# Preparing the next pair in units -1 to 5, and its conversions two units apart

## The chip, the cores and the metric

The kernel runs on one core of one Trainium2 chip. The metric is device time in microseconds (us): the time of one execution as the device measures it. The engines have short names below: TensorE is PE (its weight loads PEld), VectorE is DVE, ScalarE is ACT, GpSimd is POOL, and SyncE (SP) issues nearly all DMAs of the part that matters here.

## The reference

Three stages run one after the other; the change lies in the first.

```python
# 1. attention: batch 2, 8 heads, 768 rows, head size 64
q_bits = (einsum('bhsd,dk->bhsk', q, proj) > 0)      # 6 bits a row, a bucket number
k_bits = (einsum('bhsd,dk->bhsk', k, proj) > 0)
mask   = q_bucket[..., :, None] == k_bucket[..., None, :]
scores = where(mask, scale * q @ k.T, -1e9)
attn   = softmax(scores) @ v
# 2. mixture of experts: 1536 tokens, 8 experts of 192 tokens each, 512 -> 1024 -> 512
# 3. rms norm, then (silu(xn @ w_gate) * (xn @ w_val)) @ w_out: 512 -> 1536 -> 512
```

The three weight matrices of stage 3 arrive as 64-bit numbers. They are not needed before stage 3, but the kernel turns them into 32-bit numbers during the attention ("conversions").

## The kernel before

**Units and pairs.** The 16 heads of both batches are taken two at a time: eight pairs (0 to 7), each of six row tiles of 128 by two heads, so twelve units a pair and NU = 96 units. A unit is one head's 128 rows against all 768 keys. The loop over u issues a software pipeline: the exponential of unit u+1 (expo, L350, ACT), six transposes of the probabilities of unit u (transp, L361, PE) with their copies out of PSUM (L363 on ACT, L365 on DVE), the scores of unit u+2 (scores, L336 and L339, PE; then the row minimum L341 on DVE), half of the product with v (pv, L380, PE; copy L385, ACT), in even units the combination of a finished tile (comb, L395; comb_v, L420), and at last whatever the table fill holds for this unit. Each engine runs its own instructions in this order of issue, and SP its DMAs too; a wait holds up everything behind it on that engine. So L339 of the first tile of the next pair, issued in unit 10, must find that pair's operands ready.

**Preparing a pair.** For pair p, during pair p-1, the table holds: prep_t four times, for k and q and each half of the rows (three transposes L278, a copy by ACT, L282 or L284, then POOL's rounded part nh, L285, and rest nl, L286); prep_d after the second half of k and of q (six DMAs each, L310 to L312, that put these parts in the layout of the scores); prep_p for each half (six products with the projection, L294, then the sign comparison L297 on DVE into sg); prep_s after the second (four DMAs of the signs, L320); and in the unit behind it load_pair for the next pair but one (three DMAs, L98). SLOTS names the units: -1 and 0 for k, 1 and 3 for q, 5 and 6 for the signs. Pair 1, prepared during pair 0, has its own SLOTS1.

**Conversions.** There are 36, each of a 128 by 512 block: conv_load (one DMA of 512 KB, L242, into the wide buffer w64, of which there are three), conv (one instruction on ACT, L250; two on DVE, L253 and L254; four on POOL, L255 to L258) and conv_store (one DMA of 256 KB, L263). Conversion n stands in unit 5 + 12n/5: units 5, 7 and 9 of pair 0, 0, 2, 5, 7 and 9 of pairs 1 to 6, and 0, 2 and 5 of pair 7. Its load is issued five units earlier and its store three later. Within a unit what belongs to the preparation stands ahead of the conversion.

**PSUM.** The transposes, prep_t, prep_p and comb take their output tiles from one ring of three buffers (ps_m, tile m), so each waits until the copy out of the tile three places back is done.

Behind the attention, the routing of stage 2 begins with key work on DVE and weight splits on ACT; the 32-bit weights are read back much later.

Of the kernel before, what the change touches and what calls it, by code (L numbers as in the profile page):

```python
# [15 lines left out]
I64 = mybir.dt.int64  # L16
# [7 lines left out]
BIG = 2.0 ** 30  # L24
ACT_EVAC = 1
SLOTS1 = (0, 0, 4, 5, 5, 6)
CONV = 5
SLOTS = (-1, 0, 1, 3, 5, 6)
WSTEP = (4, 7, 9, 10, 10, 13, 15, 16)
POOL_LO = (0, 1, 4, 5, 7)  # L30
DVE_HI = (0, 4)
# [15 lines left out]
def lsh_attention__moe__swiglu_kernel(ctx, tc, q, k, v, proj, m_wg, m_w1, m_w2,  # L47
# [8 lines left out]
    TPB = S // 128  # L56
# [29 lines left out]
    cv = att.enter_context(tc.tile_pool(name="cv", bufs=2))  # L86
# [140 lines left out]
    convs = []  # L227
    for src, dst in ((f_wg, wg_d), (f_wv, wv_d), (f_wo, wo_d)):
        n = src.shape[0] * src.shape[1] // (128 * 512)
# [5 lines left out]
    def cv_at(src, i):  # L235
        per = src.shape[1] // 512
        return slice((i // per) * 128, (i // per) * 128 + 128), slice((i % per) * 512, (i % per) * 512 + 512)

    def conv_load(n):
        src, dst, i = convs[n]  # L240
        w = cv.tile([128, 512], I64, name="w64", bufs=3)
        nc.sync.dma_start(w, src[cv_at(src, i)])  # L242
        CV[n] = w

# [266 lines left out]
    def at(u, f, *a):  # L511
        fill.setdefault(u, []).append((f, a))

    for p in range(1, NPAIR):
        u0 = (p - 1) * TPB * 2
        slots = iter(SLOTS if p > 1 else SLOTS1)
        for nm in "kq":
            for half in range(2):
                n = u0 + next(slots)
                at(n, prep_t, p, nm, half)  # L520
            at(n, prep_d, p, nm)
        for half in range(2):
            n = u0 + next(slots)
            at(n, prep_p, p, half)
        at(n, prep_s, p)
        if p + 1 < NPAIR:
            at(n + 1, load_pair, p + 1)
    for n in range(len(convs)):
        u = CONV + n * 12 // 5
        at(u - 5, conv_load, n)  # L530
        at(u, conv, n)
        at(u + 3, conv_store, n)
    for i in range(8):
# [59 lines left out]
    for s in range(2):  # L593
        r = slice(64 * s, 64 * s + 64)
# [718 lines left out]
```

## Time and profile before

| what | value |
|---|---|
| median of 3 runs | 814.34 us (813.39 to 814.79) |
| the profiled execution, time | 814.53 us |
| its span, first to last instruction | 812.7 us |
| PE busy | 761.3 us, 94% |
| DVE / ACT / POOL busy | 513.7 / 398.0 / 328.6 us |
| mean granted clock of TensorE | 0.967 |
| DMA over the span | 115.58 MB, mean 142 GB/s |
| conversion loads, median from issue to landing | 5.3 to 6.4 us |

The span is cut on the page into 40 slices of 20.3 us; the attention takes the first 14 to 15 of them. Busy time of PE counts an instruction from start to modelled end, so a busy PE can still be slowed by its clock. In lists of instructions, "idle before" is the time in which the engine did nothing ahead of that instruction, and the name behind it is what ended that idle time.

### The profile page before, as it was taken

The page shows a single profiled execution, that of the slowest core. Times are in us where ns is not written, and L with a number is a line of the kernel's source. Part 1 is how long each engine was busy: PE and PEld are TensorE (multiplying, and loading weights), DVE is VectorE, ACT ScalarE, POOL GpSimd, SP SyncE. Part 2 cuts the span into 40 slices and gives each one's busy share as a digit, 9 for nine tenths or more (in the row PEclk, how much of TensorE's full clock was granted, in tenths as well). Part 3 has the DMA queues.
Part 4 walks back from the last instruction along what each step waited for, and adds up shares of the span by engine and source line. Part 5 has one row for each costly group of instructions (what it writes and reads, how often), then busy time and mean ns, then how long its engine had stood idle before and what let it go on. Part 6 is the DMA issues. An engine that isn't in the chain of part 4 may idle for free.

```text
span 812.7 us, 14759 instructions
## 1 busy us (share of the span) xinstructions
PE 761.3 (94%) x5317; PEld 685.2 (84%) x5317; DVE 513.7 (63%) x1342; ACT 398.0 (49%) x863; POOL 328.6 (40%) x309
## 2 busy tenths in 40 slices
PE   7999999999989983698999999999999999999997
PEld 3788777787878863498999999999999999999996
DVE  7788786889878878467787887766422332233222
ACT  3677765676766762265676776644211221121111
POOL 3278786877868720586767660000100010001001
PEclk8999999999999995699999999999999999999999
DMA  3578897989879612377777834363200110001001
GB/s 79 175 206 217 258 248 208 271 253 278 213 233 268 192 34 78 96 226 226 244 255 241 261 102 156 117 195 117 78 1 1 40 39 1 1 1 40 1 1 39
DMA packets 89770, 115.58 MB, mean 142 GB/s; under 512 B 22124, under 2 KB 68188, under 8 KB 89692
## 3 DMA queue, kind: packets, MB, share of 16 engines
q1 hardware_dynamic: 87612, 108.28, 44.8%
q0 software_dynamic: 1920, 6.29, 2.1%
q8 instruction: 44, 0.72, 0.4%
q14 instruction: 34, 0.28, 0.1%
q10 hardware_dynamic: 160, 0.00, 0.0%
HBM read 77.62 MB, written 18.87 MB: 119 GB/s over the span
## 4 chain that ended last, share of the span: by engine, by line
PE 37%; issue 18%; POOL 1%; DVE 1%; ACT 1%; POOLq 0%; ACTq 0%; DVEq 0%
PE pg L1194 6%; PE pv L1194 6%; PE py L1029 6%; PE po L1222 6%; PE ph L1005 6%; PE py L1031 3%; PE ph L1007 3%; POOL out_dram L1230 1%; PE ph L983 1%; PE py L1101 0%; DVE wl L218 0%; PE px L1061 0%; PE px L1084 0%; ACT bt L1015 0%; DVE yn L1091 0%
## 5 line engine op out<-in xcount | busy, mean ns | idle before, releaser
L1230 POOL DMA_INDIRECT out_dram<-ot,oi x12 | 11.7, 974 | 307.8 <-DVE ot L1228 306.2
L350 ACT ACTIVATE pr<-sc,rs 128x768 f32<-128x768 f32 x96 | 94.9, 989 | 50.4 <-DVE rs L343 31.6
L341 DVE TENSOR_REDUCE rs<-sc 128x1 f32<-128x768 f32 x96 | 91.5, 953 | 34.7 <-PE sc L339 34.2
L218 POOL TENSOR_TENSOR wl<-wr,wh 128x1024 fp32r<-128x1024 f32 x39 | 95.0, 2446 | 44.0 <-PE ph L983 20.9
L1203 DVE TENSOR_TENSOR a<-sg,pg 128x384 f32<-128x384 f32 x48 | 26.6, 553 | 103.1 <-ACT sg L1201 103.1
L361 PE MATMUL m<-ident,pr 128*128 128x128 f32 x576 | 83.4, 281 | 3.1 <-ACT pt L363 2.5
L380 PE MATMUL xo<-pt,ld_v 128*64 128x128 f32 x1128 | 82.9, 282 | 0.0
L1005 PE MATMUL ph<-xg,wh 128*128 128x384 f32 x256 | 75.3, 363 | 3.8 <-DVE ht L1022 3.1
L1029 PE MATMUL py<-ht,wh 128*128 128x384 f32 x256 | 76.7, 364 | 0.0
L361 PEld LDWEIGHTS m<-ident,pr 128*128 128x128 f32 x576 | 63.8, 141 | 15.1 <-issue 7.4
L380 PEld LDWEIGHTS xo<-pt,ld_v 128*64 128x64 f32 x1128 | 60.0, 137 | 18.6 <-issue 11.9
L1201 ACT ACTIVATE sg<-pg 128x384 f32<-128x384 f32 x48 | 23.5, 490 | 105.8 <-PE pg L1194 105.7
L1207 ACT ACTIVATE ah<-a 128x384 fp32r<-128x384 f32 x48 | 25.2, 525 | 99.3 <-DVE a L1204 99.3
L1194 PE MATMUL pg<-xh,gl 128*128 128x384 f32 x192 | 64.6, 336 | 0.0
L1194 PE MATMUL pg<-xl,gh 128*128 128x384 f32 x192 | 64.5, 336 | 0.0
L1194 PE MATMUL pg<-xh,gh 128*128 128x384 f32 x192 | 64.5, 336 | 0.0
L1194 PE MATMUL pv<-xh,vl 128*128 128x384 f32 x192 | 64.4, 335 | 0.0
L1194 PE MATMUL pv<-xl,vh 128*128 128x384 f32 x192 | 64.4, 335 | 0.0
L1194 PE MATMUL pv<-xh,vh 128*128 128x384 f32 x192 | 64.4, 335 | 0.0
L1031 PE MATMUL py<-ht,wl 128*128 128x192 f32 x256 | 63.7, 253 | 0.0
L215 ACT ACTIVATE wh<-wr 128x1024 fp32r<-128x1024 f32 x50 | 51.2, 1054 | 14.2 <-PE py L1029 11.4
L339 PE MATMUL sc<-s_k,s_q 82*128 82x384 f32 x192 | 49.9, 341 | 8.7 <-DMA s_q<-sg 8.7
(252 smaller groups left out, 1952.4 us busy)
## 6 DMA issues: line engine op xcount, KB each, us to landing
wr<-in_moe_w_dram SPq DMA_DIRECT2D x64, 512.0 KB, 4.7
w<-in_moe_w_gate_dram SPq DMA_DIRECT2D x12, 512.0 KB, 6.4
w<-in_moe_w_val_dram SPq DMA_DIRECT2D x12, 512.0 KB, 5.7
w<-in_moe_w_out_dram SPq DMA_DIRECT2D x12, 512.0 KB, 5.3
s_k<-nh_k SPq DMA_DIRECT2D x28, 192.0 KB, 3.4
s_q<-nh_q SPq DMA_DIRECT2D x28, 192.0 KB, 4.2
ld_v<-in_v_dram SPq DMA_DIRECT2D x8, 384.0 KB, 6.2
wg_d<-ha SPq DMA_DIRECT2D x12, 256.0 KB, 5.5
```

The lines of the kernel that those rows point to most:

```text
L215: nc.scalar.activation(WH[i], WR[i], AF.Copy)
L218: (nc.gpsimd if pool else nc.vector).tensor_tensor(WL[i], WR.pop(i), WH[i], op=OP.subtract)
L339: nc.tensor.matmul(ps[:, n, :HALF], q2[:64 + NS, h, qs], k2[:64 + NS, h, n * HALF:(n + 1) * HALF], start=False, stop=True)
L341: nc.vector.tensor_reduce(rs[:, h, 0:1], ps[:, :, :HALF], axis=AX.XY, op=OP.min)
L350: nc.scalar.activation(pt, ps[:, :, :HALF], AF.Exp, scale=rs[:, h, 1:2], bias=rs[:, h, 2:3], accum_out=rs[:, h, 3:4])
L361: nc.tensor.transpose(t[:, i, :], pt[:, c * 128:(c + 1) * 128], ident)
L380: nc.tensor.matmul(xo[64 * h:64 * h + 64], vt[:, h, chunk(p, c), :], a[h][:, c, :], start=(c == 0), stop=(c == TPB - 1))
L1005: hi = lambda: nc.tensor.matmul(ph[:, :2 * CAP], wh[:, d], xg[:, d].rearrange("p a b -> p (a b)"), start=(d == 0), stop=(d == KD - 1), ski ...
L1029: hi = lambda: nc.tensor.matmul(py[d][:, :2 * CAP], wh[:, ds], ht[:, f].rearrange("p a b -> p (a b)"), start=(f == 0), stop=(f == KF - 1), ...
L1031: lo = lambda: nc.tensor.matmul(py[d][:, :CAP], wl[:, ds], ht[:, f, 0], start=False, stop=False, skip_group_check=True)
L1194: nc.tensor.matmul(t[:, :TJ], a[:, d, :], b_[:, d, :], start=(n == 0), stop=(n == 3 * KD - 1))
L1222: nc.tensor.matmul(PO[j][t], a[:, ts], b_, start=(f == 0 and n == 0), stop=(f == KG - 1 and n == 2))
```

## The change

The preparation moves to units -1, 0, 1 and 2 for the transposes (the second half of q from 3 to 2) and 4 and 5 for the signs (from 5 and 6), and load_pair with it from 7 to 6. SLOTS1 stays. The conversions get a list of units for each pair: four in pairs 0, 1, 3, 5 and 6, five in pairs 2 and 4, six in pair 7, in all 36 as before. Most lie two units apart; in pairs 1, 3, 5 and 6 the first is in unit 3, in pairs 2 and 4 in unit 2. Loads of conversions in units 3 to 7 of a pair are issued two units before that pair begins, the others five units ahead, and none before the unit behind the conversion that last read its buffer; there are four wide buffers.

```diff
-CONV = 5
-SLOTS = (-1, 0, 1, 3, 5, 6)
+CONV1 = (5, 7, 9, 11)
+CONV5 = (2, 4, 6, 8, 10)
+CONV4 = (3, 5, 7, 9)
+CONVN = (0, 2, 4, 5, 7, 9)
+SLOTS = (-1, 0, 1, 2, 4, 5)
...
     def conv_load(n):
         src, dst, i = convs[n]
-        w = cv.tile([128, 512], I64, name="w64", bufs=3)
+        w = cv.tile([128, 512], I64, name="w64", bufs=4)
...
-    for n in range(len(convs)):
-        u = CONV + n * 12 // 5
-        at(u - 5, conv_load, n)
+
+    turns = [CONV1, CONV4, CONV5, CONV4, CONV5, CONV4, CONV4, CONVN]
+    units = [w * TPB * 2 + u for w, t in enumerate(turns) for u in t]
+    assert len(units) == len(convs)
+    for n, u in enumerate(units):
+
+        r = u % (TPB * 2)
+        at(max(u - r - 2 if 3 <= r < 8 else u - 5, units[n - 4] + 1 if n > 3 else 0), conv_load, n)
         at(u, conv, n)
         at(u + 3, conv_store, n)
```

## Rows read from the trace of the kernel before

**Rows 1.** The page's 40 slices of the span, busy share in tenths and granted clock.

```profile
PE   7999999999989983698999999999999999999997
...
PEclk8999999999999995699999999999999999999999
```

**Rows 2.** Table of windows, PE, pairs 1 to 7: stretch, length, busy (count), clock, DMA.

```profile
267.90:294.70 26.80, 26.80 (x256) 1.00 0.35 117
sum 240.00, PE 227.99; mean PE 32.57
```

**Rows 3.** Waits of PE in pairs 1 to 6: us in total, times, longest.

```profile
PE sc L339 <- DMA s_q<-sg: 8.7, 4, 3.0
PE m L361 <- ACT pt L363: 2.5, 6, 0.4
PE m L361 <- ACT nr_k L284: 0.6, 1, 0.6
```

**Rows 4.** Table of windows, PE, behind the wait of pair 2.

```profile
125.00:128.00 3.00, 3.00 (x19) 0.50 1.06 406
```

**Rows 5.** Timeline of PE in pair 2: start, us, instruction, [idle before <- releaser].

```profile
105.48 0.93 PE L361 MATMUL m<-ident,pr 128*128 128x128 f32 x6 [0.42 <-ACT pt L363]
...
112.65 0.82 PE L361 MATMUL m<-ident,pr 128*128 128x128 f32 x6
...
120.40 0.60 PE L336 MATMUL sc<-s_k,s_q 128*128 128x384 f32 x2
123.87 0.59 PE L339 MATMUL sc<-s_k,s_q 82*128 82x384 f32 x2 [2.87 <-DMA s_q<-sg]
```

**Rows 6.** Timeline of DVE in pair 2.

```profile
100.16 1.43 DVE L253 TENSOR_SCALAR ha<-w 128x512 int32<-128x512 int32 x1
101.51 0.72 DVE L254 TENSOR_SCALAR sg<-w 128x512 int32<-128x512 int32 x1
...
109.79 0.42 DVE L253 TENSOR_SCALAR ha<-w 128x512 int32<-128x512 int32 x1
...
112.85 0.68 DVE L297 TENSOR_SCALAR sg<-m,pm 114x384 fp32r<-114x384 f32 x1 [0.46 <-PE m L294]
```

**Rows 7.** Timeline of SP's DMA issues in pair 2.

```profile
108.19 0.60 SPq L310 DMA_DIRECT2D s_q<-nh_q  x1
...
111.74 0.61 SPq L312 DMA_DIRECT2D s_q<-nl_q  x1
...
116.22 1.71 SPq L320 DMA_DIRECT2D s_k<-sg  x2
117.97 1.59 SPq L320 DMA_DIRECT2D s_q<-sg  x2
```

**Rows 8.** Timeline of POOL in pair 2.

```profile
103.28 0.61 POOL L255 TENSOR_SCALAR ha<-ha 128x512 f32<-128x512 f32 x1
...
106.44 1.28 POOL L258 TENSOR_TENSOR ha<-ha,sg 128x512 int32<-128x512 int32 x1
107.66 0.50 POOL L285 CAST nh_q<-nr_q 128x384 fp32r<-128x384 f32 x1
108.24 1.02 POOL L286 TENSOR_TENSOR nl_q<-nr_q,nh_q 128x384 fp32r<-128x384 f32 x1
```

**Rows 9.** Timeline of all engines at the end of pair 5.

```profile
225.56 1.59 SPq L320 DMA_DIRECT2D s_q<-sg  x2
...
232.08 0.59 PE L339 MATMUL sc<-s_k,s_q 82*128 82x384 f32 x2 [3.00 <-DMA s_q<-sg]
```

**Rows 10.** Timeline of all engines at the start of pair 5.

```profile
197.87 1.14 DVE L193 TENSOR_SCALAR kl<-kl 128x48 f32<-128x48 f32 x1
...
199.62 0.52 PE L361 MATMUL m<-ident,pr 128*128 128x128 f32 x3 [0.59 <-ACT nr_k L284]
```

**Rows 11.** Table of windows, the last pair, PE, PEld, DVE, ACT, POOL in turn.

```profile
267.90:294.70 26.80, 26.80 (x256) 22.68 (x254) 22.76 (x76) 20.40 (x46) 15.81 (x15) 1.00 0.35 117
```

**Rows 12.** The page's list of DMA issues: count, size, us to landing.

```profile
w<-in_moe_w_gate_dram SPq DMA_DIRECT2D x12, 512.0 KB, 6.4
```

## The prediction

> **What bounds the kernel now.** I read the slices of the page first: TensorE (PE) is busy in nearly all of the first 14 of 40 slices, the attention, with nine tenths or more of its clock from the second slice on [rows 1]. The change touches attention alone, so the question is how much PE idles there. A table of PE by pair answers: cut at each pair's first exponential, the seven pairs from 1 on take 240.00 us and PE is busy for 227.99; the last one takes 26.80 for 11 units and has no idle time at all [rows 2]. So all 12.01 us of idle time lie in pairs 1 to 6, which take 213.20. A plain unit then costs 26.80 / 11 = 2.44 us and PE sets the pace wherever nothing holds it. PE's waits in the same stretch say what holds it: 8.7 us in four waits for the sign copies (s_q<-sg, L320) before L339, 2.5 us in six waits of 0.42 for a copy out of PSUM, 0.6 us once [rows 3]; together 11.8 of the 12.0.
>
> A wait costs more than itself once: behind the one of 2.87 us the clock, granted in full while PE was busy, fell to 0.50, the lower of its two levels (1.2 GHz), for 3 us [rows 4], and work that takes 3.0 us there takes 1.5 at the upper one, and I count 1.6 with the edges. What can be won is at most 12.0 + 1.6 = 13.6 us.
>
> Now one long wait, in pair 2. Unit 5's transposes start at 105.48, unit 7's at 112.65; at 120.40 unit 10 begins the scores of the next pair and at 121.00 it needs the copied signs, which come at 123.87 [rows 5]. The last sign half was computed by VectorE (DVE) at 112.85 to 113.53 [rows 6], yet SP issued the sign copies only from 116.22 to 119.56: from 108.19 it issues without a pause, first the six copies of q to 112.35, then stores and loads that stand in line before prep_s [rows 7]. SP began so late because the q copies need GpSimd's (POOL's) second q half, and that cast started at 107.66, straight behind a conversion that held POOL from 103.28 to 107.72 [rows 8]. So the cause is conversion, then q casts, then SP, then signs.
>
> **Prep earlier.** The changed slots put the second half of q at unit 2 instead of 3, the sign products at 4 and 5 instead of 5 and 6, and move ten of SP's copies and three loads with them. The number of instructions is the same everywhere. Call the start of unit n T(n). Before, signs were ready 0.88 us after T(7) and PE needed them 121.00 - 112.65 = 8.35 after it. After, they are ready 0.88 after T(6), and PE needs them 8.35 + 2.44 = 10.79 after it. The four issues take 119.56 - 116.22 = 3.34, and the last landed 4.31 after its issue here [rows 5, 7] and 4.93 in the longest wait (232.08 - 227.15) [rows 9]: 8.5 to 9.2 us after T(6), which is 1.6 to 2.3 us early. This needs SP free by then. With no conversion ahead of it in four of the pairs, POOL does the two instructions of the second q half in 1.60 us (107.66 to 109.26) [rows 8]; give ScalarE's (ACT's) copy before them a whole unit, 2.44, then 4.16 for six issues and 0.86 for a load (half of the 1.71 of two sign issues): SP is free 9.1 after T(3) at worst, while T(6) lies 2.44 + 7.17 = 9.6 after T(3). The 8.7 us of waits and the 1.6 of slow clock go. On SP the q copies now stand right behind the two x_d stores of the same unit, which wait for DVE's product of that unit; what that costs them lies within the worst case above. Behind prep_s stands load_pair, which leaves a unit earlier; its first reader is at unit 11. Two or three conversion loads now leave together at unit 10, ahead of the k copies of unit 0, which nobody reads for ten units. So nothing on this chain is late next within 1.6 us.
>
> **Conversions two units apart.** Each conversion is unchanged work: one ACT, two DVE, four POOL instructions. What changes is whom they meet. DVE's first one (L253) took 1.43 us at 100.16, while POOL was inside another conversion, and 0.42 at 109.79, with POOL idle [rows 6, 8]. After that slow case DVE was behind and PE waited 0.42 at 105.48 [rows 5]; that is the wait that comes six times. The slow one is the conversion of unit 2, between the q casts. In the four pairs with units 3, 5, 7, 9 it is gone; pairs 2 and 4 still have one in unit 2, so I keep 2 x 0.42 = 0.8, and 0.6 for the single wait in pair 5, which follows L193 at 1.14 us [rows 10] and has nothing to do with the slots. Retained: 1.4. POOL keeps up: 4.44 us a conversion [rows 8] against two plain units of 4.87.
>
> In words of the Trainium skill ("SBUF — State Buffer", section "Who interferes with whom") VectorE and GpSimd share a port pair as an exclusive lock, and the second to ask waits for the whole instruction of the first. The two L253 durations agree. By that rule each conversion that meets a busy GpSimd could be held twice, once per VectorE instruction; this is the second rival below.
>
> **The last pair.** It had three conversions and gets six, in units 0, 2, 4, 5, 7, 9. DVE is busy 22.76 of 26.80 us there, 4.04 free [rows 11]. Three more cost 3 x 0.84 = 2.5, with both instructions at 0.42. The one in unit 5 follows by 2.44 what holds POOL for 4.44, and those of 7 and 9 then find POOL busy too: three times 2.15 (1.43 + 0.72, by 100.16 and the one after it [rows 6]) in place of 0.84, another 3.9. That is 6.4 against 4.04 free: 2.4 over. If none of the free time can be used it is 6.4, if the three fall in gaps it is 0. I take 2.0, near the first, since DVE can catch up in the gaps before its waits for PE. POOL ends near the pair's end; nothing of the routing waits for it soon.
>
> **Four units of transposes in a row.** Units 11, 0, 1 and 2 each have three transposes more and an ACT copy more; before it was 11, 0, 1 and 3. The trace has three in a row without PE idling, and one place where PE waited 0.59 for such a copy [rows 10]. Bounds: 0, or 6 preparations x 4 x 0.59 = 14.2 (pair 1 keeps SLOTS1). I take 0.5, since the three in a row cost nothing. The fourth wide buffer and the earlier loads change no engine's work, and I take them at nothing: every conversion's load is issued five to nine units ahead, 12 us or more, where it was always five, and a load lands 6.4 us after its issue [rows 12]. Were one late, L250 would hold ACT, and the exponential behind it, for as long.
>
> **Sum.** 13.6 - 1.4 - 2.0 - 0.5 = 9.7 us less. The profiled execution took 814.53 (span 812.7), so 804.8; the median of the runs shown is 814.34, 0.2 below, so **804.6 us**. About 0.2%, 1.6 us, is what a measurement here can tell from no change.
>
> **Rivals.**
> Copies still late (0.10): the sign copies land later than 4.93 after issue because loads were put ahead of them. For it: a wide load lands 6.4 after issue [rows 12]; at 7.5 the copies come 11.7 after T(6), 0.9 late in each of six pairs, 5.5 us: 810. Against: only one wide load stands between the q copies and the signs now. The Trainium skill ("DMA: Bandwidth & Descriptors", section "Queues, rings and completion order") says each DMA engine takes descriptors in the order of its ring, which is why bytes queued ahead count; landing at 4.31 and 4.93 does not settle how much.
>
> The last pair pays (0.13): DVE is held by POOL in both instructions of the three crowded conversions and its free time is not usable: 6.4 instead of 2.0, 809. For it: DVE has 4.04 free of 26.80 [rows 11]. Against: the pair's own three conversions before cost PE nothing.
>
> All costs vanish (0.06): 13.6 less, 801 or below.
>
> No change (0.06): the signs come early but PE then waits as long elsewhere, say for the next pair's first copies, 812.7 to 816. Against: no other wait in the rows is near 8.7 us.
>
> Slower (0.07): with four transposing units in a row PE finds no free PSUM buffer, since ACT has its exponential, its copies and the new one in each. Place: units 11 to 2; price: 0.59 each [rows 10], 24 times 14.2 us, in all 814.3 - 13.6 + 1.4 + 2.0 + 14.2 = 818.3. The gain is used up at 10.2 / 0.59, some 17 of the 24, and from 20 on it is slower by more than 0.2%. Against: units 11, 0 and 1 in a row made PE wait in no pair but the fifth [rows 3].
>
> My forecast has 0.58, for 801 to 807.5. Faster is 0.58 + 0.10 + 0.13 + 0.06 = 0.87, within 0.2% 0.06, slower 0.07. A range of 800.8 to 811.0 takes in the forecast and the two rivals above it; it leaves out the gain's edge, no change and slower, 0.19.
>
> **What would show it.** Right: no wait of PE on L339 for s_q<-sg over 0.3 us; prep_s issued by SP about 1 us after the second L297, with a pause before it; six pairs near 33 us; L253 near 0.42 but in the last pair and in unit 2; no stretch at 0.50 before the attention's end. Wrong: L339 still waits; PE waits for nr_k or nr_q copies or for pt in units 11 to 5; the last pair over 29 us; ACT held at L250 by a load that is not there.

## The result and the profile after

The changed kernel takes **801.74 us** (median of 4 runs, 800.46 to 801.89) where the kernel before took 813.87 (813.26 to 814.79): a ratio of 0.9847, 95% interval 0.983 to 0.9864. That is 12.1 us less. The forecast was 804.6, in a range of 800.8 to 811.0; the sign is right, the gain larger than said. The profiled execution took 801.59 us, its span is 799.7 (before 812.7), so the two traces differ by 13.0. In experiments 2, 3 and 9 below, one run each took 858 to 932 us at a lower mean clock (0.75 to 0.83); the ratios leave it out, and it moves the medians by at most 0.4 us. Code lines of the attention stand three lower in the changed file: L339 is now L342, L361 is L364, L250 (ACT) is L253, L253 (DVE) is L256, L297 is L300, L320 is L323.

The slices of the page, which answer to [rows 1], no longer have the 8 in the twelfth slice, where the wait at the end of pair 5 was [rows 9]:

```profile
PE   7999999999999954889999999999999999999997
...
PEclk9999999999999975899999999999999999999999
```

The table of windows by pair (stretch, length, PE busy with count, clock, DMA share, GB/s) answers to [rows 2, 11]; of the seven stretches these are the fifth pair, the last, and the sum:

```profile
186.20:220.40 34.20, 33.27 (x304) 1.00 0.84 256
...
253.10:281.50 28.40, 26.85 (x254) 1.00 0.43 150
sum 226.60, PE 224.03; mean PE 32.00
```

PE's idle time in these pairs went from 12.01 us to 226.60 - 224.03 = 2.57, and 1.55 of it lies in the last pair. What is left has other names than in [rows 3] (PE's waits, us in total, times, longest):

```profile
PE m L364 <- DVE pt L368: 2.1, 2, 1.2
PE m L364 <- ACT pr L353: 0.3, 1, 0.3
```

In these stretches no wait for the sign copies remains and none above 0.1 us for ACT's copies out of PSUM, and the clock is 1.00 in all seven stretches. Cut more finely, from one unit's first transpose (L364) to the next's, the 13.0 us come from these places:

| place | before | after | difference |
|---|---|---|---|
| unit 10, six pairs (the wait for the signs, and the start of the slow clock in pair 2) | 26.33 | 15.31 | -11.0 |
| units 2 to 6, six pairs | 92.8 | 88.7 | -4.2 |
| unit 11, six pairs (rest of the slow clock in pair 2: 3.73 to 2.69) | 17.56 | 16.83 | -0.7 |
| all other units of the six pairs | 76.4 | 76.9 | +0.5 |
| last pair, 11 units | 26.19 | 28.55 | +2.4 |

Pair 2 again, SP and then PE, answering to [rows 7, 5]:

```profile
105.45 0.61 SPq L315 DMA_DIRECT2D s_q<-nl_q  x1
106.16 0.75 SPq L245 DMA_DIRECT2D w<-in_moe_w_gate_dram  x1
108.42 1.71 SPq L323 DMA_DIRECT2D s_k<-sg  x2
110.18 1.60 SPq L323 DMA_DIRECT2D s_q<-sg  x2
```

```profile
107.51 0.82 PE L364 MATMUL m<-ident,pr 128*128 128x128 f32 x6
...
118.25 0.51 PE L342 MATMUL sc<-s_k,s_q 82*128 82x384 f32 x2
```

Here SP is done with the q copies at 106.06 and pauses from 106.91 to 108.42, until the signs exist. The last of the four issues ends 111.78 - 107.51 = 4.27 us after unit 6 began, and L342 starts 10.74 after it, without a wait. Pairs 4, 5 and 6 are like this. In pair 3 the last issue ends 4.9 us after unit 6 began, and in pair 1, where POOL's k casts stand behind the conversion of unit 11 of pair 0, 7.5 us after it; L342 does not wait there either.

Most of the last pair's loss, 1.84 of 2.36 us, is in one place. DVE and POOL around its unit 6, and PE behind them:

```profile
269.91 1.28 POOL L260 TENSOR_TENSOR ha<-ha,lr 128x512 int32<-128x512 int32 x1
270.11 1.37 DVE L256 TENSOR_SCALAR ha<-w 128x512 int32<-128x512 int32 x1
...
271.26 1.35 POOL L261 TENSOR_TENSOR ha<-ha,sg 128x512 int32<-128x512 int32 x1
271.39 1.50 DVE L257 TENSOR_SCALAR sg<-w 128x512 int32<-128x512 int32 x1
...
273.42 0.55 PE L364 MATMUL m<-ident,pr 128*128 128x128 f32 x3 [1.24 <-DVE pt L368]
...
275.79 0.44 PE L364 MATMUL m<-ident,pr 128*128 128x128 f32 x2 [0.32 <-ACT pr L353]
```

The conversion of unit 5 meets that of unit 4 on POOL. Both DVE instructions start just behind the start of a POOL instruction and last 1.37 and 1.50 us in place of 0.42 each; DVE's copy L368 comes late, and PE's unit 7 takes 4.15 us where it took 2.31. The other 0.5 us come at the pair's end.

### The profile page after: what moved, and what is told of

It is laid out like the page before. It is cut to its first block, busy times and chain, and to the rows that moved or that the text cites. A ratio compares the mean times of both kernels' runs of the same rounds, so it can differ in the third digit from the quotient of the medians.

```text
span 799.7 us, 14773 instructions
## 1 busy us (share of the span) xinstructions
PE 758.3 (95%) x5317; PEld 685.1 (86%) x5317; DVE 510.5 (64%) x1342; ACT 397.9 (50%) x863; POOL 329.5 (41%) x309
## 4 chain that ended last, share of the span: by engine, by line
PE 37%; issue 18%; DVE 1%; POOL 1%; ACT 1%; POOLq 0%; ACTq 0%; DVEq 0%
PE pg L1202 6%; PE pv L1202 6%; PE py L1037 6%; PE po L1230 6%; PE ph L1013 5%; PE py L1039 3%; PE ph L1015 3%; POOL out_dram L1238 1%; PE ph L991 1%; PE py L1109 0%; DVE wl L221 0%; PE px L1069 0%; PE px L1092 0%; ACT bt L1023 0%; ACT sq L1055 0%
## 5 line engine op out<-in xcount | busy, mean ns | idle before, releaser
L1238 POOL DMA_INDIRECT out_dram<-ot,oi x12 | 11.7, 977 | 307.7 <-DVE ot L1236 306.2
L364 PE MATMUL m<-ident,pr 128*128 128x128 f32 x576 | 82.1, 278 | 2.9 <-DVE pt L368 2.1
L364 PEld LDWEIGHTS m<-ident,pr 128*128 128x128 f32 x576 | 63.4, 140 | 13.7 <-issue 5.3
L218 ACT ACTIVATE wh<-wr 128x1024 fp32r<-128x1024 f32 x50 | 51.1, 1053 | 13.8 <-PE py L1037 11.4
L366 ACT ACTIVATE pt<-m 128x384 f32<-128x384 f32 x120 | 55.7, 487 | 4.1 <-PE m L364 3.7
```

The costliest lines, as they stand in the source:

```text
L218: nc.scalar.activation(WH[i], WR[i], AF.Copy)
L364: nc.tensor.transpose(t[:, i, :], pt[:, c * 128:(c + 1) * 128], ident)
L366: nc.scalar.activation(o[:, 3 * half:3 * half + 3, :], t, AF.Copy)
```

## The experiments

Each run is shown with its edit. Every time is a median and stands beside the kernel before on the same chip, whose medians lie between 814.9 and 816.3.

**1. The slots alone** (kernel before, new SLOTS).

```diff
-SLOTS = (-1, 0, 1, 3, 5, 6)
+SLOTS = (-1, 0, 1, 2, 4, 5)
```

> The kernel before with the new slots alone; its conversions stay in units 0, 2, 5, 7 and 9, with three wide buffers. Order theory (the second half of q now stands ahead of the conversion of unit 2 in GpSimd's queue, and the signs a unit earlier, so the copies of the signs arrive before PE asks for them): the waits on s_q<-sg are gone, 12 us, the short waits behind the conversion of unit 2 stay, the last pair loses nothing: 801 to 803. Spacing theory (only conversions kept out of the preparation free GpSimd and VectorE): the conversion of unit 0 still stands ahead of the q casts, SP stays late, half or more of the waits stay: 808 or above.

Measured: 804.18 us, ratio 0.9861 (0.9829 to 0.9892), a little over what was expected. PE's waits in the pairs:

```profile
PE m L294 <- ACT pt L363: 2.6, 5, 0.5
PE m L361 <- ACT nr_k L284: 0.6, 1, 0.6
```

The signs are never late. But the crowded conversion is still there (POOL's last conversion instruction, then DVE's two):

```profile
99.16 1.28 POOL L258 TENSOR_TENSOR ha<-ha,sg 128x512 int32<-128x512 int32 x1
99.28 1.45 DVE L253 TENSOR_SCALAR ha<-w 128x512 int32<-128x512 int32 x1
...
100.65 0.72 DVE L254 TENSOR_SCALAR sg<-w 128x512 int32<-128x512 int32 x1
```

Unit 4 takes 4.33 us here and 3.71 after the whole change, in every pair: 0.62 x 6 = 3.7 us that only the new places of the conversions win. The last pair stays at 26.19.

**2. The conversions alone** (changed kernel, old SLOTS).

```diff
-SLOTS = (-1, 0, 1, 2, 4, 5)
+SLOTS = (-1, 0, 1, 3, 5, 6)
```

> The changed kernel with the old slots (second half of q in unit 3, signs in 5 and 6); conversions two units apart. Order theory: signs are 0.88 us after unit 7 begins, copied 8.5 to 9.2 us after it, wanted 8.35 after it: 0.2 to 0.9 us late in the four pairs with conversions in 3, 5, 7, 9, and 1.5 to 3.7 in the two with one in unit 2, which again stands ahead of the q casts. With 0.3 us of PE time more at each wait than its idle time shows: 6 to 11 us above the changed kernel, 808 to 812. Spacing theory: no waits, 801 to 803.

Measured: 804.53 us, ratio 0.9863 (0.9826 to 0.9899), between the two expectations and nearer to the lower, so I was wrong here: this half alone is worth as much as the other. PE's waits name the signs once:

```profile
PE m L364 <- DVE pt L368: 1.8, 2, 1.2
PE sc L342 <- DMA s_q<-sg: 1.5, 1, 1.5
```

In five of the six pairs the last sign issue ended 7.9 to 8.0 us after the start of unit 6, and the first L342 started 3.8 to 4.1 us after that without waiting. With POOL free for the q casts, SP is free in time, and in these five pairs the copies land sooner than the 4.31 to 4.93 us that I had from [rows 7, 9]. In pair 2, which does wait, it is 5.6. Gains of about 11.4 and 11.1 for the halves and 12.1 for both (by the pair times of the traces 10.2, 9.8 and 13.0) do not add: each half by itself removes nearly all of the sign waits.

**3. The last pair's six conversions at even units.**

```diff
-CONVN = (0, 2, 4, 5, 7, 9)
+CONVN = (0, 2, 4, 6, 8, 10)
```

> The changed kernel with the last pair's six conversions in units 0, 2, 4, 6, 8, 10 instead of 0, 2, 4, 5, 7, 9. Crowding theory (VectorE is held by GpSimd where conversions are one unit apart, 1.37 and 1.50 us instead of 0.42 each): the wait of 1.24 and the one of 0.32 go, unit 7 of that pair falls from 4.15 to 2.31 us; the conversion of unit 10 may cost up to 1 us at the tail: 800.0 to 800.9. Load theory (six conversions are simply too much for VectorE in 12 plain units): no change, 801.7.

Measured: 799.88 us, ratio 0.9812 (0.9776 to 0.9848), 0.1 below what was expected. The last pair by the windows (PE, PEld, DVE, ACT, POOL busy in turn):

```profile
253.10:279.60 26.50, 26.50 (x253) 22.38 (x252) 23.84 (x78) 21.47 (x47) 21.82 (x22) 1.00 0.51 163
```

PE has no idle time there although six conversions remain, and by its units the pair costs 26.50 in place of 28.55, with a wait of 0.24 at its very end. So, for the attention, it was not the number of conversions but the two that follow each other by one unit. The total does not show this as cleanly. The conversion of unit 10 is now the crowded one, and it ends beside the start of the routing:

```profile
281.49 1.34 POOL L261 TENSOR_TENSOR ha<-ha,sg 128x512 int32<-128x512 int32 x1
281.62 1.50 DVE L257 TENSOR_SCALAR sg<-w 128x512 int32<-128x512 int32 x1
```

From the pair's last transposes to the first of stage 2 (L991) this trace takes 43.7 us, where the changed kernel and experiment 4 take 42.3: most of what the pair wins is lost again there. From L991 to the end it takes 1.5 us less than the changed kernel, whose profiled execution has a stretch at the lower clock in stage 2 (0.50 from 357.4 to 360.6) that this one has not. The edit does not touch that stage.

**4. Three conversions in the last pair, five in each of pairs 2 to 6.**

```diff
-CONVN = (0, 2, 4, 5, 7, 9)
+CONVN = (0, 2, 5)
...
-    turns = [CONV1, CONV4, CONV5, CONV4, CONV5, CONV4, CONV4, CONVN]
+    turns = [CONV1, CONV4, CONV5, CONV5, CONV5, CONV5, CONV5, CONVN]
```

> The changed kernel with five conversions (2, 4, 6, 8, 10) in all of pairs 2 to 6 and three in the last (0, 2, 5). Crowding theory: the last pair is back at 26.2 us from its first to its last unit (28.55 now), the pairs with five cost no more than those with four (in the changed kernel both take 32.7): 799.2 to 800.0. If a fifth conversion costs what it did with the old slots (0.70 us a pair): 801 to 802.

Measured: 798.15 us, ratio 0.9791 (0.9758 to 0.9823), 1.0 below the lowest expectation. The last pair is back at 26.19, and the pairs with five conversions cost what those with four do, but for 0.4 in pair 3. One wait of 0.9 is left, at the end of pair 4. At the end of the attention this trace is 1.8 us ahead of the changed kernel's, which is what was expected; the other 1.5 are the same stretch of slow clock in stage 2, which is missing here too: at that place the changed kernel's trace falls 1.6 further behind.

**5 and 6. The sign copies one and two units later** in the table, with load_pair behind them (d = 1, then d = 2).

```diff
-        at(n, prep_s, p)
+        d = 1 if p > 1 else 0
+        at(n + d, prep_s, p)
         if p + 1 < NPAIR:
-            at(n + 1, load_pair, p + 1)
+            at(n + d + 1, load_pair, p + 1)
```

> The changed kernel with the four copies of the signs, and the load of the next pair behind them, put one unit later (unit 6 instead of 5). My margin: the copies land 8.5 to 9.2 us after unit 6 begins and are wanted 10.8 after it. One unit later SP issues them from some 2.4 us later: 0.1 to 0.9 us late in each of six pairs, with 0.3 more in PE time each: 804 to 809. If the margin is wider than I worked out (2.5 us or more): no wait, 801.7.

> The same copies two units later (unit 7). By my margin 2.5 to 3.3 us late in each of six pairs, 0.3 more each, and a stretch at half clock behind the longer ones: 17 to 25 us, 819 to 827, slower than the kernel before. If the margin is a unit wider: 0.1 to 0.9 late, 804 to 809.

Measured: 802.49 us, ratio 0.9862 (0.982 to 0.9904), and 801.29, ratio 0.9848 (0.9806 to 0.9889). Neither has a wait for signs, and neither tests the margin: the last sign issue ended at most 1.0 us later than in the changed kernel. A unit in the table only orders SP's queue. Where nothing that stands ahead waits, SP issues the copies as soon as their data exist, whatever unit they were put in.

**7. The signs behind a store that waits.** Taught by this, I put prep_s in unit 9 but left load_pair, so that a conversion's store, which waits for POOL, stands ahead of the signs.

```diff
-        at(n, prep_s, p)
+        d = 4 if p > 1 else 0
+        at(n + d, prep_s, p)
```

> The kernel after with one step displaced: for pairs 2 to 7 prep_s (the four sign copies) is issued four units later, in unit 9, so that in SP's queue it stands behind the store of the conversion in unit 5, which waits for POOL. Everything else stays. My theory (what is won in the change is the time of the sign copies' issue, and the margin is some 2 us): in the four pairs with conversions in units 3, 5, 7, 9 the last issue comes about T(6)+9.5 instead of T(6)+4.27, lands 3 to 4.5 later, and the first L342 waits 2 to 3.3 us; with 0.3 us more of PE time behind each, and a slow clock behind some, 9 to 15 us are lost: 811 to 817. In pairs 2 and 4 the store ends earlier and little or nothing is waited for. Rival (the signs' time has nothing to do with it; what is won comes from the conversions' places): 801 to 802.5, no wait over 0.5.

Measured: 821.49 us, ratio 1.0087 (1.0061 to 1.0113), some 20 us above the changed kernel, slower than before, and above the 811 to 817 expected. PE's waits for the signs return:

```profile
PE sc L342 <- DMA s_q<-sg: 7.9, 4, 3.3
PE sc L342 <- issue: 6.7, 1, 6.7
```

The longest is in pair 1 (the trace names no releaser for it, only "issue"), where the last issue ended at 87.03 (85.14 + 1.89); L342 came at 92.76, and the six microseconds behind it ran at the lower level of the clock (1.2 GHz; window as above):

```profile
85.14 1.89 SPq L323 DMA_DIRECT2D s_q<-sg  x2
...
92.76 0.98 PE L342 MATMUL sc<-s_k,s_q 82*128 82x384 f32 x2 [6.75 <-issue]
```

```profile
92.80:95.80 3.00, 3.00 (x17) 0.50 0.87 350
...
95.80:98.80 3.00, 3.00 (x14) 0.50 0.03 12
```

Nothing but the place of the sign copies was changed, so their time does decide, with 14.6 us of waits turning into 21.2 us of pair time. Which pairs pay was not as I had it. In pairs 3, 5 and 6 the last issue ended at 9.7 us after unit 6, as expected, but L342 came 1.3 to 2.3 us later and the unit lost only 0.3 to 1.3. In pairs 2 and 4 the issue ended earlier, at 9.43 and 8.93, and L342 came 4.8 and 5.2 later, with 3.7 and 3.4 lost. The mean DMA share from the first sign issue to L342 was 0.94 and 1.02 in pairs 2 and 4, and 0.92, 0.78 and 0.62 in pairs 3, 5 and 6. The two late pairs have the highest shares, but 0.92 and 0.94 stand beside landings of at most 1.6 and 4.8 us, so the share alone does not explain them; which transfer does it was not tried.

**8. Three wide buffers, loads five units ahead** (as in the kernel before, the rest of the change kept).

```diff
-        w = cv.tile([128, 512], I64, name="w64", bufs=4)
+        w = cv.tile([128, 512], I64, name="w64", bufs=3)
...
-        at(max(u - r - 2 if 3 <= r < 8 else u - 5, units[n - 4] + 1 if n > 3 else 0), conv_load, n)
+        at(max(u - 5, units[n - 3] + 1 if n > 2 else 0), conv_load, n)
```

> The changed kernel with three wide buffers and every conversion load five units ahead, as before the change. My step: loads ahead and the fourth buffer are worth nothing, 801.7, and no wait of ACT at L253 for a load. Rival: a load lands late (6 us and more when several are queued) and holds ACT, and with it PE, in some units: 804 or above.

Measured: 808.44 us, ratio 0.9925 (0.9894 to 0.9956), 6.7 us above the changed kernel. SP and ACT in pair 1:

```profile
68.14 0.61 SPq L315 DMA_DIRECT2D s_k<-nh_k  x1
...
69.81 0.94 SPq L245 DMA_DIRECT2D w<-in_moe_w_gate_dram  x1
```

```profile
78.37 0.67 ACT L253 ACTIVATE lr<-w 128x512 int32<-128x512 uint32 x1 [4.11 <-DMA w<-in_moe_w_gate_dram]
```

The load that belongs to unit 0 stands behind six k copies that wait for POOL's casts (64.38 to 68.75), and POOL is in the conversion that the new list puts in unit 11 of pair 0. It is issued at 69.81, ACT waits 4.11 us for it, the exponential behind it is late, and pair 1 takes 37.84 in place of 32.92. Three more kernels split the edit.

**9. Four buffers, loads five units ahead:**

```diff
-        at(max(u - r - 2 if 3 <= r < 8 else u - 5, units[n - 4] + 1 if n > 3 else 0), conv_load, n)
+        at(u - 5, conv_load, n)
```

> The kernel after with its four wide buffers, but every load issued five units before its conversion (as in the kernel before). Theory lead (the loss with three buffers came from loads issued late or from their place in SP's queue, behind the copies of the preparation): the same wait of ACT at the conversion's first instruction in pair 1 (4.1 us with three buffers), 806 to 809. Theory buffer (the fourth buffer alone was what mattered): as after, 801 to 802.5, and no ACT wait over 1 us for a wide load.

**10. Three buffers, loads ahead** as far as the buffers allow:

```diff
-        w = cv.tile([128, 512], I64, name="w64", bufs=4)
+        w = cv.tile([128, 512], I64, name="w64", bufs=3)
...
-        at(max(u - r - 2 if 3 <= r < 8 else u - 5, units[n - 4] + 1 if n > 3 else 0), conv_load, n)
+        at(max(u - r - 2 if 3 <= r < 8 else u - 5, units[n - 3] + 1 if n > 2 else 0), conv_load, n)
```

> The kernel after with three wide buffers, and its loads ahead as in the change, but none before the unit behind the conversion that last read the buffer (which is one conversion nearer than with four). Theory lead: most loads leave at the same unit as with four, two units before the pair, or only a little later, and the time is that of after or up to 1.5 us over it, 801 to 803. Theory buffer: 806 to 809, as with three buffers and loads five units ahead.

**11. Three buffers, loads five units ahead, but first in their unit's list:**

```diff
-        w = cv.tile([128, 512], I64, name="w64", bufs=4)
+        w = cv.tile([128, 512], I64, name="w64", bufs=3)
...
-        at(max(u - r - 2 if 3 <= r < 8 else u - 5, units[n - 4] + 1 if n > 3 else 0), conv_load, n)
+        fill.setdefault(max(u - 5, units[n - 3] + 1 if n > 2 else 0), []).insert(0, (conv_load, (n,)))
```

> The kernel with three wide buffers and loads five units ahead, which lost 6.7 us to the kernel after, with one thing changed: each load stands first among the DMAs of its unit's table list, ahead of the preparation's copies, which wait for POOL. Theory place in the queue (the load in unit 0 of pair 1 was late because it stood behind six copies that waited): the ACT wait of 4.1 us in pair 1 goes, 801 to 803.5. Theory lead (five units are too few whatever stands ahead): 806 to 809.

Measured for 9, 10 and 11: 810.1 us, ratio 0.9944 (0.9911 to 0.9976); 801.86, ratio 0.9835 (0.977 to 0.9901); 804.25 (802.15 to 806.15), ratio 0.9879 (0.9813 to 0.9944). With four buffers and late loads ACT waits as with three, the longest time at the next load of pair 1:

```profile
84.21 0.68 ACT L253 ACTIVATE lr<-w 128x512 int32<-128x512 uint32 x1 [3.76 <-DMA w<-in_moe_w_gate_dram]
```

So the fourth buffer by itself shows no gain and the earlier loads are what holds the gain. With the load first in its list SP issues it before it comes to the k copies:

```profile
53.13 0.43 SPq L245 DMA_DIRECT2D w<-in_moe_w_gate_dram  x1
```

16.7 us earlier than 69.81, at the same five units; the wait of ACT in pair 1 is gone, and that pair takes 33.39. The place in the queue explains that wait. The median stays 2.5 above the changed kernel's, with a spread of 4.0 over four runs; two sign waits of 1.6 us together came back in its trace (pairs 1 and 3), where loads now stand elsewhere among the copies.

**12. The first keys of the routing moved** (experiment 4 and one line).

```diff
-    at(HP * TPB * 2 + 10, keys, 0)
+    at(NU - 8, keys, 0)
```

> The kernel with five conversions in each of pairs 2 to 6 and three in the last (798.15 us), with one more edit: the first key instructions of the routing on DVE (L196) are issued in unit 88, in the last pair, where POOL has little to do, instead of unit 58, the end of pair 4, beside a conversion. Theory (the 0.9 us wait of PE at the end of pair 4 is DVE held by POOL at L196): that unit falls from 3.8 to about 2.7, the last pair stays at 26.2, 796.5 to 797.6. Rival (the work only moves, and the last pair or the start of the routing waits for it): 798 to 798.6.

Measured: 798.03 us (797.01 to 798.62), ratio 0.9768 (0.9732 to 0.9803). Unit 11 of pair 4 takes 2.71, the last pair 26.19, and PE does not wait at all in the pairs: the mechanism is as said. The total is not told apart from experiment 4. At the end of the attention this trace is 1.32 us ahead, and it loses 1.6 at one place of stage 2 that the edit does not touch. Both kernels wait there the same time, first experiment 4 and then this one:

```profile
354.93 0.44 PE L1013 MATMUL ph<-xg,wh 128*128 128x384 f32 x1 [2.11 <-DVE ht L1030]
```

```profile
353.70 0.45 PE L1013 MATMUL ph<-xg,wh 128*128 128x384 f32 x1 [2.09 <-DVE ht L1030]
```

but behind the wait the granted clock is 1.00 in the one and 0.54 in the other (windows of PE):

```profile
355.80:358.80 3.00, 3.00 (x23) 1.00 0.74 237
```

```profile
355.80:358.80 3.00, 3.00 (x14) 0.54 0.74 223
```

## Why the prediction was right, and where it was off

**What bounds the kernel** was right: PE, with idle time in pairs 1 to 6 for one main reason. The chain conversion, q casts, SP, signs was right too, and stronger than I had it: free either end of it (experiments 1 and 2) and the waits go; delay the signs (experiment 7) and they come back.

**Prep earlier** was right in its timing: I gave 4.22 and 10.79 us after T(6) for the last issue and for the need, and 4.27 and 10.74 came in pair 2, and the same within 0.1 in pairs 4 to 6; pairs 1 and 3 had the issue later and the margin covered it. The margin of 1.6 to 2.3 us was too small. In experiment 2, with the issue 3.6 us later, five pairs still did not wait. My landing times of 4.31 and 4.93 are no property of the copy, as experiment 7 shows.

**The term that was mis-sized** is the first, "at most 13.6 us" from idle time and slow clock. The pairs gained 15.4 and had 11.7 in my sum (13.6 - 1.4 - 0.5). With 2.4 lost in the last pair that makes the 13.0 of the traces, where I had 9.7. A wait costs PE more than the idle time the trace puts in front of it: the one wait for signs of experiment 10 is 0.78 in the trace, and its unit is 1.02 longer; the 1.50 of experiment 2 costs 1.74; the 3.00 of [rows 9] cost 3.24. It is 0.24 us more for each, and why is not shown. The sign waits in [rows 3] are 8.7 us, and the units 10 shrank by 11.0: the surcharge of four waits, 0.55 of slow clock, and 0.85 in pairs 4 and 6, where the trace has waits of 0.1 only, make up the rest. The slow clock itself was sized rightly: unit 11 of pair 2 gave back 1.04, and at the end of unit 10 the same products took 1.43 in place of 0.88 us, together 1.6.

```profile
118.96 0.88 PE L380 MATMUL xo<-pt,ld_v 128*64 128x128 f32 x12
...
124.63 1.43 PE L380 MATMUL xo<-pt,ld_v 128*64 128x128 f32 x12
```

**The 0.8 kept for pairs 2 and 4** was wrong. I had tied the slow L253 (now L256) to unit 2. It belongs to what POOL does: before, the conversion of unit 0 was still on POOL. In the changed kernel the one of unit 2 is the first in its pair, finds POOL free, and is short:

```profile
98.18 0.42 DVE L256 TENSOR_SCALAR ha<-w 128x512 int32<-128x512 int32 x1
98.52 0.49 DVE L257 TENSOR_SCALAR sg<-w 128x512 int32<-128x512 int32 x1
```

Each of the six pairs had a slow one, of 1.28 to 1.46 us (that of pair 2 in [rows 6]); now no L256 in them lasts over 0.63. Units 2 to 6 give 4.2 us, where the six waits of 0.42 add to 2.5. The Trainium skill ("SBUF — State Buffer", section "Who interferes with whom") says that the second to ask for the port pair that VectorE shares with GpSimd waits for a whole instruction of the first. This case's trace agrees: 1.37 and 1.50 us beside POOL's 1.28 and 1.35, and 0.42 with POOL free.

**The key wait**, 0.6 kept, stayed as a cost, somewhat larger: it now stands as 0.9 at the end of pair 4, and without it, in experiment 12, that unit is 1.05 shorter. It moves between pair 4 and pair 5 in experiments 5, 6 and 11, with the sum of the two pairs unchanged (66.94 and 66.97).

**The last pair** was sized near enough, 2.0 against 2.36, but as three crowded conversions; it is one, that of unit 5, for 1.84, and 0.5 at the end. That the size came out is in part luck.

**Four units of transposes in a row**, 0.5: no PE wait for nr_k or nr_q is left, so nothing shows for it.

**Loads and the fourth buffer, "nothing"**: right for the buffer (801.86 without it, 801.74 with it), wrong for the loads. Without their lead the same change gives 808 to 810. My reason, that five units had always been enough, counted time in units, 12 us, while SP issues when what stands ahead is done. The forecast did not suffer, since the change has the lead in it.

The rivals: copies still late did not happen, though the time from issue to use does spread, up to 5.7 us in experiment 7. The last pair paid, but a third of the 6.4. The slower end, no free PSUM buffer, did not happen.

## What to carry to other kernels

Find the chain behind a repeated wait and see how many of its links can be freed; two edits that free the same chain do not add, so try each alone. Place a DMA by what stands ahead of it in its issuing queue, not by how many loop steps it is early. And put conversions that share VectorE and GpSimd at least as far apart as GpSimd needs for one: one unit of 2.4 us was too near for 4.4 us of POOL's work, and two units apart PE did not wait, save behind the last conversion of experiment 3.

## What the hardware showed that I had not expected

The same sign copies came to use between 1.3 and 5.7 us after the end of their issue in one run. The same idle time of 2.1 us in stage 2 was followed by the full clock in one run (experiment 4) and by 0.54 of it for 3 us in another (experiment 12), which is worth 1.6 us of the total. That is as large as the smaller effects studied here, and part of the gains in total time of experiments 3 and 4 is no more than this.
